# Another order of the block products, and of the sums before them, in the first and last of four matrix stages

## The chip, the cores and the metric

One Trainium2 chip, one core. The metric is the device time of one execution in microseconds (us), the median of several runs. TensorE (PE in the profile) multiplies and has its own row for loading weights (PEld); VectorE (DVE) and ScalarE (ACT) work elementwise; GpSimd (POOL) and SyncE (SP) mostly issue DMAs here.

## The reference

`x` is 2048 x 1024. Two branches are mixed row by row with a gate:

```python
g = _sigmoid((x * gate_w).sum(-1, keepdims=True))
# branch A
a = jnp.einsum("bsd,ed->bse", x, dft_hid_re)
b = jnp.einsum("bsd,ed->bse", x, dft_hid_im)
A = jnp.einsum("ts,bse->bte", dft_seq_re, a) - jnp.einsum("ts,bse->bte", dft_seq_im, b)
# branch B
h = _layernorm(x, axis=-1)
u = _gelu(jnp.einsum("bsd,sf->bdf", h, w1) + b1)
B = (jnp.einsum("bdf,fs->bds", u, w2) + b2).transpose(0, 2, 1)
return g * A + (1 - g) * B
```

The hidden width F is 3584; everything is float32.

## The kernel before, in words

Four large matrix products run one after the other as four stages, each a class: **Fourier** (name `q`: the sequence transform applied to x), **Mixed** (`y`: the hidden transform, written to the output with gate and bias), **Up** (`u`: layernormed x times w1, then gelu) and **Down** (`o`: u times w2, added onto the output with the gate). Fourier comes first and Down last; both the results of Fourier (`q`) and of Up (`u`) go through DRAM to the stage behind.

Each stage sees its product as a 4 x 4 grid of big blocks (16 of them) times a 4 x 2 grid of small blocks (8), which gives 8 output blocks. Instead of the 32 block products of the ordinary rule it takes the 26 of a fast scheme in the manner of Strassen. SCHEME (L49) has a row for each: which big blocks, with sign, are summed for one operand, which small ones for the other, and to which output blocks the product is added. ORDER is the order in which a stage takes the 26 rows, SUMS names partial sums that may be made on the way to an operand.

`plan` (L522) goes through the rows in that order. It makes each needed sum out of two that are at hand, choosing the cheapest pair: a block or sum that was used within the last `keep` products is still in SBUF; an older sum was stored to DRAM when made and is loaded again; a block of the input is loaded again. Where two rows in a row have the same small operand (`again`, L601), its split is kept. So the order decides how many loads, stores and sums there are and when each falls due.

Each operand is split (`split_into`, L508) into a high part, made by ScalarE (L509), and a low part, the rest, made by VectorE (L514 or L516), so that three float32r matmuls of 128 x 128 by 128 x 512 (L775 to L777) stand for a float32 product. The sums are VectorE's (`add` L479, `sub` L482); in Mixed and Down a few are made by an accumulating DMA issued from POOL (`add_onto`, L490). A product is 4 x 4 x 2 x 3 = 96 matmuls in Fourier and 7 x 4 x 3 = 84 in Down. In Fourier the big operand is 1024 wide and the small one 512, in Down both are 512; a sum or a split of a product takes four instructions in Fourier (4 slices of the contraction) and seven in Down.

A product runs through its slices k, over all its PSUM banks at each (8 in Fourier, 4 in Down, of 8 there are); the last two slices are taken together. Where the output signs of a product and of the next one agree enough, the next goes on in the same banks (`chained`, L613 to L619), and only the output blocks whose coefficient changes are read in between (`reads`, L620). A read is a first copy into SBUF by ScalarE or VectorE, whichever is free (`plain_copy`, L812 or L814), or an add onto the block by VectorE (`fused`, L820), one instruction a bank. A block that isn't read again for more than `gap` products is finished: in Fourier stored (L495), or accumulated onto its stored first part by DMA (L900); in Down scaled by ScalarE (L1037) and accumulated onto the output by DMA (L1039), but for those which the last product ends: they are loaded, added onto with the gate as scale, and stored by SP.

The order of all instructions is fixed when the kernel is built. Graph (L284) holds every load, sum, split, matmul group, copy and store as a task with a key, roughly its due time in slices, and the engines that can do it; `schedule` (L323) plays them through with an assumed duration for each, takes the ready task with the lowest key on each engine, and gives out the buffers: 40 of 128 x 1024 ("f"), 23 of 128 x 512 ("h") and 8 PSUM banks. The matmuls keep the order in which they are built. Loads go through SP's queue, most stores and all accumulating DMAs through POOL's. In product 1 of Fourier the saved sums are stored by SP. From product 12 of Fourier on, the statistics of the 16 row tiles of x are made beside it (`STATS_AT`, L206).

Of the kernel before, what the change touches and what calls it, by code (L numbers as in the profile page):

```python
# [44 lines left out]
def signs(words):  # L45
    return [[(c == "+") - (c == "-") for c in word] for word in words]
# [54 lines left out]
    '.-.-...+',  # L101
    '..+--+..',
])
Q_ORDER = [5, 14, 23, 3, 7, 11, 21, 22, 18, 24, 6, 17, 0, 13, 9, 8, 19, 15, 12, 2, 20, 25, 1, 16, 10, 4]
Q_SUMS = signs([
    '+.+.............',
    '.............+.+',
# [7 lines left out]
    '.....+.......+..',  # L115
    '+...........+...',
    '......+...+.....',
    '.+.+............',
    '.+.+.....+......',
    '.+.+.--...-.....',  # L120
    '.+.+.....+.+....',
    '....+...+.......',
    '....+-..+....-.-',
    '....+..++.......',
    '....+..++..+....',
    '+-..........+..+',
    '+-.......-..+..+',
    '......+...+.+..+',
    '......+...+.+.++',
    '....+..+........',  # L130
    '+.+.-..-..+.....',
    '..+.......+..+.+',
    '..+.......+..+++',
]), SMALL_SUMS
Q_PERM = ((0, 1, 2, 3), (0, 1, 2, 3), (0, 1))
# [69 lines left out]

STATS_AT, STATS_STEP = ("q", 12), 3  # L206
H_LEAD, H_EACH = 25, 1.3
O_ORDER = [24, 6, 17, 15, 0, 13, 12, 2, 25, 1, 16, 10, 5, 14, 4, 23, 3, 7, 11, 21, 18, 22, 9, 8, 19, 20]
O_SUMS = signs([
    '+.+.............',  # L210
    '.............+.+',
# [7 lines left out]
    '.....+.......+..',  # L219
    '+...........+...',  # L220
    '......+...+.....',
    '....+...+.......',
    '....+-..+....-.-',
    '....+..++.......',
    '....+..++..+....',
    '.+.+............',
    '.+.+.....+......',
    '.+.+.--...-.....',
    '.+.+.....+.+....',
    '..+.......+...+.',  # L230
    '..+.......+..+++',
    '....+..+........',
    '+.+.-..-..+.....',
    '............+.++',
    '......+...+.+.++',
    '+........-..+..+',
    '+-.......-..+..+',
]), SMALL_SUMS


# [171 lines left out]
def gated_mix_kernel(  # L412
# [411 lines left out]
    class Fourier(Bilinear):  # L824
        gap = Q_GAP

        def __init__(self):
            super().__init__("q", 4, 4, 2, H, D, "R", {"R": 1, "W": 2}, Q_ORDER, Q_SUMS, Q_PERM)

# [163 lines left out]
    class Down(Bilinear):  # L993
# [4 lines left out]
        def __init__(self):  # L998
            super().__init__("o", 7, 4, 1, H, H, "W", {"W": O_KEEP, "R": O_KEEP}, O_ORDER, O_SUMS, O_PERM)

# [197 lines left out]
```

## Time and profile before

| | |
|---|---|
| median of 3 runs | 1852.84 us (1852.65 to 1852.87) |
| profiled execution, its own time | 1853.4 us |
| span from its first to its last instruction | 1851.6 us |
| instructions | 24397 |
| granted TensorE clock | 1.000 |
| DMA | 491.88 MB, 266 GB/s mean |
| Fourier, about | 5 to 570 us |
| Down, about | 1352 to 1847 us |

The profile is of one execution. An engine's busy time counts its own instructions, not the issuing of DMAs by SP or the waits. Rows of groups give line, engine, operation, output and inputs, shape and count, then busy us and mean ns of one, then the idle time before them and what ended most of it. Rows of windows give for a stretch of time its length, then the busy us and the instructions of PE, PEld, DVE, ACT and POOL, the granted clock, the busy share of the DMA engines, and GB/s. Rows of a timeline give start and duration in us. Matmuls are pipelined: the starts are the ones to go by.

### The profile page before, as it was taken

The page shows a single profiled execution, that of the slowest core. Times are in us where ns is not written, and L with a number is a line of the kernel's source. Part 1 is how long each engine was busy: PE and PEld are TensorE (multiplying, and loading weights), DVE is VectorE, ACT ScalarE, POOL GpSimd, SP SyncE. Part 2 cuts the span into 40 slices and gives each one's busy share as a digit, 9 for nine tenths or more (in the row PEclk, how much of TensorE's full clock was granted, in tenths as well). Part 3 has the DMA queues.
Part 4 walks back from the last instruction along what each step waited for, and adds up shares of the span by engine and source line. Part 5 has one row for each costly group of instructions (what it writes and reads, how often), then busy time and mean ns, then how long its engine had stood idle before and what let it go on. Part 6 is the DMA issues. An engine that isn't in the chain of part 4 may idle for free.

```text
span 1851.6 us, 24397 instructions
## 1 busy us (share of the span) xinstructions
PE 1845.6 (100%) x8122; PEld 1524.0 (82%) x8122; DVE 1684.5 (91%) x2444; ACT 911.4 (49%) x1406; POOL 244.1 (13%) x416
## 2 busy tenths in 40 slices
PE   9999999999999999999999999999999999999999
PEld 7888888888888888888888888888888888888887
DVE  8899679989979999999988699899789999998995
ACT  5443335644535545586554325345455535444542
POOL 0100010111022101112121111121120000001111
PEclk9999999999999999999999999999999999999999
DMA  9967478879698667989658798796998576775974
GB/s 372 343 238 265 145 259 315 325 266 393 212 315 303 224 224 238 328 289 343 230 189 290 258 356 326 272 399 230 351 317 276 168 205 210 228 208 134 280 203 97
DMA packets 199870, 491.88 MB, mean 266 GB/s; under 512 B 24832, under 2 KB 24832, under 8 KB 199744
## 3 DMA queue, kind: packets, MB, share of 16 engines
q1 hardware_dynamic: 161712, 373.91, 58.5%
q0 software_dynamic: 37888, 116.16, 19.3%
q8 instruction: 63, 1.03, 0.2%
q14 instruction: 63, 0.52, 0.1%
q10 hardware_dynamic: 144, 0.26, 0.0%
HBM read 375.41 MB, written 114.82 MB: 265 GB/s over the span
## 4 chain that ended last, share of the span: by engine, by line
PE 84%; DVE 6%; issue 4%; DMA 4%; POOL 1%; SPq 0%; ACT 0%; POOLq 0%; DVEq 0%; ACTq 0%
PE ps_q_p L777 10%; PE ps_q_p L775 10%; PE ps_q_p L776 10%; PE ps_u_p L775 9%; PE ps_u_p L777 9%; PE ps_u_p L776 9%; PE ps_o_p L775 7%; PE ps_o_p L777 7%; PE ps_o_p L776 7%; PE ps_y_p L775 2%; PE ps_y_p L777 2%; PE ps_y_p L776 2%; DMA o_W_p<-in_w_dram 2%; DMA y_W_p<-y_W 1%; DVE o_p_r L516 1%
## 5 line engine op out<-in xcount | busy, mean ns | idle before, releaser
L777 PE MATMUL ps_q_p<-q_p_r_hi,q_p_w_lo 128*128 128x512 f32 x824 | 320.7, 389 | 0.1
L775 PE MATMUL ps_q_p<-q_p_r_hi,q_p_w_hi 128*128 128x512 f32 x824 | 320.6, 389 | 0.0
L776 PE MATMUL ps_q_p<-q_p_r_lo,q_p_w_hi 128*128 128x512 f32 x824 | 320.5, 389 | 0.0
L775 PE MATMUL ps_o_p<-o_p_r,o_p_w 128*128 128x512 f32 x728 | 283.5, 389 | 0.1
L776 PE MATMUL ps_o_p<-o_p_r,o_p_w 128*128 128x512 f32 x728 | 283.2, 389 | 0.0
L777 PE MATMUL ps_o_p<-o_p_r,o_p_w 128*128 128x512 f32 x728 | 283.2, 389 | 0.0
L775 PE MATMUL ps_u_p<-u_p_r_hi,u_p_w_hi 128*128 128x512 f32 x728 | 283.2, 389 | 0.0
L776 PE MATMUL ps_u_p<-u_p_r_lo,u_p_w_hi 128*128 128x512 f32 x728 | 283.2, 389 | 0.0
L777 PE MATMUL ps_u_p<-u_p_r_hi,u_p_w_lo 128*128 128x512 f32 x728 | 283.2, 389 | 0.0
L777 PEld LDWEIGHTS ps_q_p<-q_p_r_hi,q_p_w_lo 128*128 128x128 f32 x824 | 154.7, 188 | 32.7 <-DVE q_p_w_lo L514 0.6
L776 PEld LDWEIGHTS ps_q_p<-q_p_r_lo,q_p_w_hi 128*128 128x128 f32 x824 | 154.7, 188 | 32.1
L775 PEld LDWEIGHTS ps_q_p<-q_p_r_hi,q_p_w_hi 128*128 128x128 f32 x824 | 154.7, 188 | 32.0
L509 ACT ACTIVATE q_p_r_hi<-q_R_p 128x1024 fp32r<-128x1024 f32 (+1 forms) x101 | 104.4, 1047 | 132.6 <-DVE q_R_p L479 75.7
L509 ACT ACTIVATE o_p_w<-o_W_p 128x512 fp32r<-128x512 f32 x182 | 111.5, 627 | 113.3 <-DVE o_W_p L479 42.7
L509 ACT ACTIVATE u_p_w_hi<-u_W_p 128x896 fp32r<-128x896 f32 x104 | 97.5, 949 | 135.1 <-DVE u_W_p L479 95.2
L775 PE MATMUL ps_y_p<-y_p_r,y_p_w 128*128 128x512 f32 x416 | 162.2, 390 | 0.6 <-ACT y_c L812 0.4
L777 PE MATMUL ps_y_p<-y_p_r,y_p_w 128*128 128x512 f32 x416 | 161.9, 389 | 0.0
L776 PE MATMUL ps_y_p<-y_p_r,y_p_w 128*128 128x512 f32 x416 | 161.9, 389 | 0.0
L775 PEld LDWEIGHTS ps_o_p<-o_p_r,o_p_w 128*128 128x128 f32 x728 | 136.7, 188 | 29.3 <-DVE o_c L820 1.0
L776 PEld LDWEIGHTS ps_o_p<-o_p_r,o_p_w 128*128 128x128 f32 x728 | 136.7, 188 | 28.5
L777 PEld LDWEIGHTS ps_u_p<-u_p_r_hi,u_p_w_lo 128*128 128x128 f32 x728 | 136.7, 188 | 28.5
L776 PEld LDWEIGHTS ps_u_p<-u_p_r_lo,u_p_w_hi 128*128 128x128 f32 x728 | 136.7, 188 | 28.3
(149 smaller groups left out, 3260.7 us busy)
## 6 DMA issues: line engine op xcount, KB each, us to landing
q_R_p<-in_ct_dram SPq DMA_DIRECT2D x131, 512.0 KB, 7.1
u_W_p<-in_w_dram SPq DMA_DIRECT2D x136, 448.0 KB, 6.4
o_W_p<-in_w_dram SPq DMA_DIRECT2D x196, 256.0 KB, 5.3
o_R_p<-u SPq DMA_DIRECT2D x140, 256.0 KB, 5.0
u<-u_c POOLq DMA_DIRECT2D x126, 256.0 KB, 5.9
y_W_p<-q SPq DMA_DIRECT2D x99, 256.0 KB, 5.2
q<-q_c POOLq DMA_DIRECT2D x80, 256.0 KB, 5.6
q_W_p<-in_x_dram SPq DMA_DIRECT2D x75, 256.0 KB, 6.9
```

Source lines behind the costliest of these rows:

```text
L509: g.add({"ACT": act(v.n)}, key, lambda e: nc.scalar.activation(hi.ap, v.ap, AF.Copy, scale=-1.0 if negate else 1.0), r=(v.reg,), w=(hi.reg,))
L516: nc.vector.tensor_sub(lo.ap, v.ap, hi.ap.bitcast(F32))
L775: nc.tensor.matmul(bank.ap, wh.ap[:, c], rh.ap[:, e], start=a, stop=False, skip_group_check=True)
L776: nc.tensor.matmul(bank.ap, wh.ap[:, c], rl.ap[:, e], start=False, stop=False, skip_group_check=True)
L777: nc.tensor.matmul(bank.ap, wl.ap[:, c], rh.ap[:, e], start=False, stop=b, skip_group_check=True)
```

## The change

Q_ORDER with Q_SUMS, for Fourier, and O_ORDER with O_SUMS, for Down, are replaced; nothing else is. The scheme, the number of products, the matmuls, the tiles, the keep and gap values and the two middle stages' tables stay as they are. In Fourier rows 24, 6, 17, 15 come first, then 5, 14, 23, 3, 7, 11; the last eight rows (12 to 4) keep their places. In Down the order is new from the first row to the last. The partial sums that differ are those that suit the new order.

```diff
--- before.py
+++ after.py
@@ -101,7 +101,7 @@
     '.-.-...+',
     '..+--+..',
 ])
-Q_ORDER = [5, 14, 23, 3, 7, 11, 21, 22, 18, 24, 6, 17, 0, 13, 9, 8, 19, 15, 12, 2, 20, 25, 1, 16, 10, 4]
+Q_ORDER = [24, 6, 17, 15, 5, 14, 23, 3, 7, 11, 21, 18, 22, 9, 8, 19, 0, 13, 12, 2, 20, 25, 1, 16, 10, 4]
 Q_SUMS = signs([
     '+.+.............',
     '.............+.+',
@@ -115,21 +115,21 @@
     '.....+.......+..',
     '+...........+...',
     '......+...+.....',
-    '.+.+............',
+    '.+.......+......',
     '.+.+.....+......',
-    '.+.+.--...-.....',
     '.+.+.....+.+....',
+    '+-.......-..+..+',
     '....+...+.......',
     '....+-..+....-.-',
     '....+..++.......',
     '....+..++..+....',
-    '+-..........+..+',
-    '+-.......-..+..+',
-    '......+...+.+..+',
+    '...+.--...-.....',
+    '.+.+.--...-.....',
+    '............+.++',
     '......+...+.+.++',
     '....+..+........',
     '+.+.-..-..+.....',
-    '..+.......+..+.+',
+    '.............+++',
     '..+.......+..+++',
 ]), SMALL_SUMS
 Q_PERM = ((0, 1, 2, 3), (0, 1, 2, 3), (0, 1))
@@ -205,7 +205,7 @@
 
 STATS_AT, STATS_STEP = ("q", 12), 3
 H_LEAD, H_EACH = 25, 1.3
-O_ORDER = [24, 6, 17, 15, 0, 13, 12, 2, 25, 1, 16, 10, 5, 14, 4, 23, 3, 7, 11, 21, 18, 22, 9, 8, 19, 20]
+O_ORDER = [5, 0, 13, 14, 23, 4, 17, 24, 6, 19, 15, 3, 7, 11, 21, 22, 9, 8, 20, 12, 2, 25, 1, 16, 10, 18]
 O_SUMS = signs([
     '+.+.............',
     '.............+.+',
@@ -219,22 +219,22 @@
     '.....+.......+..',
     '+...........+...',
     '......+...+.....',
-    '....+...+.......',
-    '....+-..+....-.-',
+    '....+..+........',
+    '+.+.-..-..+.....',
     '....+..++.......',
     '....+..++..+....',
     '.+.+............',
     '.+.+.....+......',
     '.+.+.--...-.....',
     '.+.+.....+.+....',
-    '..+.......+...+.',
+    '+..+........+..+',
+    '+-.......-..+..+',
+    '....+-.......-.-',
+    '....+-..+....-.-',
+    '.............+++',
     '..+.......+..+++',
-    '....+..+........',
-    '+.+.-..-..+.....',
     '............+.++',
     '......+...+.+.++',
-    '+........-..+..+',
-    '+-.......-..+..+',
 ]), SMALL_SUMS
 
 
```

## The prediction

> **What bounds the kernel now.** I read the page first, then TensorE's timeline from end to end, then the time windows, then the timelines of VectorE around each place where TensorE stopped. The page:
>
> ```profile
> span 1851.6 us, 24397 instructions
> PE 1845.6 (100%) x8122; PEld 1524.0 (82%) x8122; DVE 1684.5 (91%) x2444; ACT 911.4 (49%) x1406; POOL 244.1 (13%) x416
> ```
>
> TensorE is busy all the time, but ends of matmuls are modelled, so I look at the starts instead. TensorE's timeline (start, duration, line) at the beginning and at the end; 54 rows lie between the last two:
>
> ```profile
> 1.19 4.45 PE L1133 MATMUL pw<-warm 128*128 128x512 bf16 x10 [1.19 <-DVE warm L1131]
> 5.25 1.66 PE L876 MATMUL ps_q_p<-q_p_r_hi,q_p_w_hi 128*128 128x512 f32 x4
> ...
> 1834.76 0.39 PE L776 MATMUL ps_o_p<-o_p_r,o_p_w 128*128 128x512 f32 x1
> ...
> 1847.22 0.39 PE L777 MATMUL ps_o_p<-o_p_r,o_p_w 128*128 128x512 f32 x1
> ```
>
> In 12.46 us there are 55 steps: 0.2266 us a matmul. The program has 26 products of 96 + 48 + 84 + 84 matmuls, 8112 besides the 10 of the warm-up, so 8111 steps from 5.25 take at least 1838 us and would end at 1843.3; the last starts at 1847.2. **About 4 us** is all that TensorE loses between its first and last real matmul. Three of the stops lie in the stages that change (Fourier and Down); for each, the matmul before and after it:
>
> ```profile
> 39.42 0.39 PE L776 MATMUL ps_q_p<-q_p_r_lo,q_p_w_hi 128*128 128x512 f32 x1
> 39.95 0.50 PE L777 MATMUL ps_q_p<-q_p_r_hi,q_p_w_lo 128*128 128x512 f32 x1
> ...
> 1486.74 0.39 PE L777 MATMUL ps_o_p<-o_p_r,o_p_w 128*128 128x512 f32 x1
> 1487.14 0.50 PE L775 MATMUL ps_o_p<-o_p_r,o_p_w 128*128 128x512 f32 x1
> ...
> 1791.70 0.39 PE L777 MATMUL ps_o_p<-o_p_r,o_p_w 128*128 128x512 f32 x1
> 1792.19 0.50 PE L775 MATMUL ps_o_p<-o_p_r,o_p_w 128*128 128x512 f32 x1
> ```
>
> Start to start less 0.227, and 0.11 for the longer next one (0.50 for 0.39): 0.41, 0.28 and 0.37 us, **1.1 us together**. The rest is in Mixed, as the groups of weight loads show (last figure: idle time before them, and its releaser):
>
> ```profile
> L775 PEld LDWEIGHTS ps_y_p<-y_p_r,y_p_w 128*128 128x128 f32 x416 | 78.1, 188 | 18.1 <-DVE y_c L820 1.0 <-ACT y_c L812 0.9
> L777 PEld LDWEIGHTS ps_y_p<-y_p_r,y_p_w 128*128 128x128 f32 x416 | 78.1, 188 | 16.3
> ```
>
> 18.1 less 16.3 is 1.8 us, waits for an evacuation of PSUM. So the kernel is bound by TensorE's count of matmuls, which no order changes. A gain is at most the 1.1 us of Fourier and Down, or 2.9 with Mixed. The start (first loads and splits, to 5.25) and the end keep their shapes.
>
> **The two ways in which TensorE can stop.** Operands late (39.95), or an evacuation late. A "chained" product goes on in the PSUM banks of the one before; where those are also read, it must wait for the readers. VectorE around the stop at 1487.14:
>
> ```profile
> 1481.61 2.48 DVE L820 SCALAR_TENSOR_TENSOR o_c<-ps_o_p,o_c 128x512 f32<-128x512 f32 x4
> 1484.00 0.68 DVE L514 SCALAR_TENSOR_TENSOR o_p_w<-o_W_p,o_p_w 128x512 fp32r<-128x512 f32 x1
> 1484.60 2.48 DVE L820 SCALAR_TENSOR_TENSOR o_c<-ps_o_p,o_c 128x512 f32<-128x512 f32 x4
> ```
>
> Two blocks of four banks are added onto; the last add ends at 1487.08, and the matmul starts at 1487.14. I place it by counting 19.04 us a product (84 x 0.2266) back from the end: it opens product 7 of Down.
>
> **Is VectorE close to the bound?** Busy time by stage, then two full slices, then the POOL, ACT and DVE groups that I use:
>
> ```profile
> 5.00:570.00 565.00, 564.86 (x2489) 467.30 (x2488) 504.96 (x652) 267.48 (x402) 63.95 (x113) 1.00 0.80 290
> 1352.40:1847.40 495.00, 494.88 (x2182) 408.93 (x2180) 461.89 (x759) 235.86 (x400) 48.50 (x64) 1.00 0.72 212
> ```
>
> ```profile
> 113.00:135.00 22.00, 22.00 (x99) 18.23 (x98) 22.00 (x30) 9.36 (x14) 0.54 (x1) 1.00 0.71 238
> 1390.40:1409.50 19.10, 19.10 (x86) 15.71 (x85) 19.10 (x32) 14.41 (x26) 1.09 (x2) 1.00 0.83 270
> ```
>
> ```profile
> L495 POOL DMA_DIRECT2D q_W<-q_W_p x16 | 8.9, 554 | 203.2 <-DVE q_W_p L482 191.8 <-DVE q_W_p L479 11.1
> L900 POOL DMA_DIRECT2D q<-q_c x8 | 6.8, 856 | 14.8 <-ACT q_c L812 14.2 <-DVE q_c L814 0.6
> L495 POOL DMA_DIRECT2D o_W<-o_W_p x7 | 3.8, 543 | 6.7 <-DVE o_W_p L479 6.2 <-DVE o_R_p L482 0.2 <-issue 0.2
> L490 POOL DMA_DIRECT2D o_W_p<-in_w_dram x14 | 12.4, 886 | 259.3 <-DMA o_c<-out_dram 60.0 <-DVE o_p_w L514 47.9 <-DVE o_p_w L516 35.3
> L812 ACT ACTIVATE o_c<-ps_o_p 128x512 f32<-128x512 f32 x23 | 13.7, 597 | 16.2 <-PE ps_o_p L777 15.9
> L814 DVE TENSOR_SCALAR o_c<-ps_o_p 128x512 f32<-128x512 f32 x5 | 3.5, 690 | 1.5 <-ACT o_c L812 1.1 <-PE ps_o_p L777 0.4
> L820 DVE SCALAR_TENSOR_TENSOR q_c<-ps_q_p,q_c x168: 679/686/693, 84.1 to 572.6; 128x512 f32<-128x512 f32 x168
> ```
>
> VectorE is spare for 60 us of 565 in Fourier and 33 us of 495 in Down. Filled, it ends 32 instructions of Down in 19.10 us, **0.60 us each** though each lasts 0.69; a 1024-wide one costs about twice, say 1.14. In 113 to 135 VectorE has no idle time and TensorE loses none: operands are made ahead, and what counts is by how much.
>
> **The change, part by part.** The counts come from the rules of plan (L522) and operand (L691), followed over both sets of tables.
>
> Fourier: sums 72 and 112 as before. Input loads fall from 76 to 72 (256 KB) and 132 to 128 (512 KB), reloads of saved sums from 28 to 20 and 20 to 16, their stores from 24 to 16 and 20 to 16. Blocks added onto in SBUF fall from 168 instructions to 160 (8 x 0.60 = 4.8 us of VectorE less); first copies rise from 72 to 88, shared by ACT and VectorE. Two more blocks are written in two parts, so accumulating DMAs rise from 8 to 24: 16 x 0.86 = 13.7 us of POOL, less 8 saved-sum stores there at 0.55, so +9.3 on 64 busy of 565. Behind them in POOL's queue stand other stores of blocks and sums. Products 18 to 25 keep their order, so every block that Mixed reads ends where it did, block 0 one product earlier. VectorE's demand, summed product by product, differs from before by 0 through product 2, -18 to -28 us at 4, 6 and 7, +9.6 at most (12), then -4 to -14. Counting 21.76 us a product from 5.25, the last operand of product 12 is made 28 us ahead now, and the nearest misses are product 1 (the stop at 39.95) and product 15:
>
> ```profile
> 340.39 0.69 DVE L516 TENSOR_TENSOR q_p_w_lo<-q_W_p,q_p_w_hi 128x512 fp32r<-128x512 f32 x1
> ```
>
> It ends 1.5 us before use (342.6), and becomes 14 us easier. Fourier therefore keeps its 0.41 (products 0 and 1 have the same shape) and gains no stop.
>
> Down: sums on VectorE 182 + 125 become 186 + 126, adds onto blocks 104 become 108: +9 x 0.60 = **5.4 us of 33 spare**. Saved sums stored 21 -> 35, loaded 21 -> 35, input loads 210 + 140 -> 210 + 126, sums made by DMA 15 -> 10. On POOL that is 14 x 0.543 less 5 x 0.886, +3.2 us on 48.5; behind these in its queue are only other stores and the accumulations of finished blocks. DMA engines are 0.72 busy there. The demand in instructions per product (seven a sum, seven a split, four a block added from the product before) is now 14, 42, 20, 21, 24, 44, 25, 36, 37, 21, 38, 28, 18, 32, 29, 24, 24, 38, 29, 36, 30, 34, 25, 31, 31, 36; it becomes 14, 21, 44, 31, 25, 21, 38, 18, 32, 45, 21, 24, 38, 29, 36, 32, 21, 25, 36, 21, 36, 38, 25, 38, 31, 36. At 32 a product VectorE is full. The running difference is 7.8 and 8.4 us at products 3 and 4, 9.6 at 15, 5.4 at 23 to 25. Against it stand the leads. The last low half of W of product 1, and the last of all 182:
>
> ```profile
> 1379.22 0.68 DVE L514 SCALAR_TENSOR_TENSOR o_p_w<-o_W_p,o_p_w 128x512 fp32r<-128x512 f32 x1
> ...
> 1825.73 0.68 DVE L516 TENSOR_TENSOR o_p_w<-o_W_p,o_p_w 128x512 fp32r<-128x512 f32 x1
> ```
>
> They are used 13.6 us into products 1 and 25, at 1384.8 and 1841.8: leads of 4.9 and 15.4. The same count over all 26 gives 10 to 31 elsewhere. Subtracting the running difference, the smallest leads after are 9.3 (product 2), 10 (3) and **8.8** (24). No operand comes late.
>
> What is left in Down is evacuation. Chained products that follow a reading: 14 now, 16 after; at 0.65 us for 14 that is 0.75. New is one of **three** blocks, after product 0: twelve copies of 0.60. TensorE's last pass takes 1.36 us a bank and its next needs bank 3 at 7.5 us from that pass's start. ACT and VectorE together, three copies a bank in under 1.36, end at about 7.2 (no cost); ACT alone ends at 1.4 + 7.2 = 8.6 (1.1 late). I take 0.4.
>
> Sum: -0.41 + 0.41 in Fourier, 0 in Mixed and Up, +0.1 + 0.4 in Down: span 1852.1. The profiled execution took 1853.4 for its 1851.6; the median of the runs is 1852.84, which I move by the same 0.5: **1853.3 us**.
>
> [...] POOL issues more DMAs, and its busy rows stand above. [...]
>
> **Rivals.** (1) *Slower by the triple copy.* If ACT does its usual share (23 of 28 copies now, so 9.6 of 12) with a split between every two, it ends 1.4 + 9.6 x 1.2 = 12.9 us after the pass began: 5.4 late, **1858.3**. It decides once copies end later than 7.5. For: VectorE's queue at 1484 did put a split between the adds. Against: the two-block copy after product 1 shows no stop. Chance 0.12. (2) *Slower by a hole in the loads.* VectorE runs short in Down even now:
>
> ```profile
> 1676.00:1695.10 19.10, 19.10 (x86) 15.82 (x85) 17.27 (x30) 8.74 (x15) 3.83 (x5) 1.00 0.68 135
> 1695.10:1714.10 19.00, 19.00 (x85) 15.74 (x84) 14.92 (x25) 7.49 (x12) 0.98 (x2) 1.00 0.40 127
> 1714.10:1733.20 19.10, 19.10 (x85) 15.80 (x85) 17.27 (x29) 11.59 (x19) 3.99 (x5) 1.00 1.00 259
> 1733.20:1752.20 19.00, 19.00 (x85) 15.76 (x84) 17.62 (x30) 8.30 (x15) 2.76 (x4) 1.00 1.03 294
> ```
>
> That is 1.8 + 4.1 + 1.8 + 1.4 = 9.1 us idle in a row. The same at products 1 to 4 or 21 to 24 is just covered by 8.8; one twice as deep costs 18.2 - 8.8 = 9.4, **1862.7**. It decides above 8.8. Against: fewer blocks are open at once (6 for 8 in Down, 5 for 6 in Fourier), which leaves more buffers for loads. Chance 0.16. (3) *Faster:* all stops of Fourier and Down go, **1851.8**; with Mixed's, 1849.9. Still within 0.2%. Chance 0.12. My forecast, with small stops moved about: 0.60.
>
> **Numbers.** 0.2% (3.7 us) is about what a measurement of this kernel can tell from no change. Faster by more needs more than the 2.9 us of stops that exist: 0.02, out of (3), for what I don't see. Slower by more is (1) and (2): 0.28. Within: 0.70. The range goes from 1850.8, most of Fourier's, Mixed's and Down's stops gone, to 1860, which takes in (1) and the smaller holes of (2); about 0.15 is left out. The forecast's own range is 1851.8 to 1855.
>
> **What would show it.** Right: starts 0.227 apart throughout, stops only at chained boundaries, the count of L900 at 24, DVE's instructions in Down up by 9, o_W stores 28. Wrong: a stop of more than 1 us at 1371 (triple copy), or one ended by a split's low half in products 2 to 4 or 21 to 25 of Down (a lead that I overrated), or any stop in Fourier after product 2.

## The result, and the profile after

The changed kernel takes **1856.24 us** (median of 22 runs, 1854.58 to 1859.10), the kernel before 1852.67 (22 runs, 1852.13 to 1853.92): a ratio of 1.0021, with a 95% interval from 1.0015 to 1.0027. That is 3.6 us: slower clear of the noise, at the very edge of the 0.2% (3.7 us) that the prediction set as its bound, and seven times the 0.5 us that it forecast. The spread has grown from 1.8 to 4.5 us, which the forecast did not have at all. The first profile of the changed kernel is of its fastest execution: 1854.58 us, span 1852.8.

The head of its page, then the groups whose counts were forecast:

```profile
span 1852.8 us, 24399 instructions
PE 1845.2 (100%) x8122; PEld 1523.1 (82%) x8122; DVE 1694.1 (91%) x2463; ACT 908.4 (49%) x1404; POOL 255.7 (14%) x433
```

```profile
L900 POOL DMA_DIRECT2D q<-q_c x24 | 20.6, 863 | 84.4 <-DVE q_c L820 69.6 <-ACT q_c L812 14.6 <-issue 0.2
L495 POOL DMA_DIRECT2D o_W<-o_W_p x28 | 15.2, 545 | 87.3 <-DVE o_W_p L479 70.9 <-DMA o_W_p<-in_w_dram 12.7 <-DVE o_Ws L479 3.6
```

The work is what was counted: 24 accumulating stores in Fourier, 28 stores of saved sums of w2 in Down. The time has gone elsewhere. TensorE's timeline at its beginning (the warm-up, then the first product) and in the first pass of Down's product 1, where banks 2 and 3 are taken over from product 0:

```profile
1.19 4.45 PE L1133 MATMUL pw<-warm 128*128 128x512 bf16 x10 [1.19 <-DVE warm L1131]
6.33 1.19 PE L876 MATMUL ps_q_p<-q_p_r_hi,q_p_w_hi 128*128 128x512 f32 x4 [0.69 <-ACT q_p_r_hi L509]
...
1371.50 0.39 PE L777 MATMUL ps_o_p<-o_p_r,o_p_w 128*128 128x512 f32 x1
1372.18 0.50 PE L775 MATMUL ps_o_p<-o_p_r,o_p_w 128*128 128x512 f32 x1 [0.29 <-ACT o_c L812]
1372.52 0.40 PE L776 MATMUL ps_o_p<-o_p_r,o_p_w 128*128 128x512 f32 x1
1372.76 0.40 PE L777 MATMUL ps_o_p<-o_p_r,o_p_w 128*128 128x512 f32 x1
1374.11 0.50 PE L775 MATMUL ps_o_p<-o_p_r,o_p_w 128*128 128x512 f32 x1 [0.95 <-DVE o_c L814]
```

Two things stand out against before. The first real matmul starts at 6.33 us where it started at 5.25. And after product 0 of Down TensorE stops twice, for 0.68 - 0.23 + 0.11 = 0.56 and 1.35 - 0.23 + 0.11 = 1.23 us: **1.8 us** at the copy of three blocks. Before's stops at 39.95, 1487 and 1792 are gone, and the last matmul starts at 1848.25 for 1847.22. So this execution is 1.0 us behind the profiled one of before, while the medians are 3.6 apart: before's profiled execution (1853.4) was 0.7 over its median and this one 1.7 under its own. The rest must be in what differs from one execution to the next.

### The profile page after: what moved, and what is told of

Same layout as the page of the kernel before. It is cut to its first block, busy times and chain, and to the rows that moved or that the text cites. A ratio compares the mean times of both kernels' runs of the same rounds, so it can differ in the third digit from the quotient of the medians.

```text
span 1852.8 us, 24399 instructions
## 1 busy us (share of the span) xinstructions
PE 1845.2 (100%) x8122; PEld 1523.1 (82%) x8122; DVE 1694.1 (91%) x2463; ACT 908.4 (49%) x1404; POOL 255.7 (14%) x433
## 4 chain that ended last, share of the span: by engine, by line
PE 99%; DVE 1%; ACT 0%; DMA 0%; issue 0%; ACTq 0%
PE ps_q_p L777 10%; PE ps_q_p L776 10%; PE ps_q_p L775 10%; PE ps_u_p L775 9%; PE ps_u_p L777 9%; PE ps_u_p L776 9%; PE ps_o_p L775 9%; PE ps_o_p L776 9%; PE ps_o_p L777 9%; PE ps_y_p L775 5%; PE ps_y_p L776 5%; PE ps_y_p L777 5%; PE ps_q_p L876 0%; DMA q_W_p<-in_x_dram 0%; DVE o_c L814 0%; ACT o_c L812 0%
## 5 line engine op out<-in xcount | busy, mean ns | idle before, releaser
L509 ACT ACTIVATE q_p_r_hi<-q_R_p 128x1024 fp32r<-128x1024 f32 (+1 forms) x105 | 108.9, 1049 | 126.2 <-DVE q_R_p L479 88.2
L775 PEld LDWEIGHTS ps_u_p<-u_p_r_hi,u_p_w_hi 128*128 128x128 f32 x728 | 136.6, 188 | 28.3
```

The costliest lines, as they stand in the source:

```text
L509: g.add({"ACT": act(v.n)}, key, lambda e: nc.scalar.activation(hi.ap, v.ap, AF.Copy, scale=-1.0 if negate else 1.0), r=(v.reg,), w=(hi.reg,))
L775: nc.tensor.matmul(bank.ap, wh.ap[:, c], rh.ap[:, e], start=a, stop=False, skip_group_check=True)
```

## The experiments

Two theories were tried against each other: **A**, that the loss lies in Down, in the triple copy; **B**, that it lies in Fourier, and varies. All times below are medians of 10 or 11 runs; the kernel before ran beside each group of four (1852.44, 1852.44 and 1852.72 us). The 95% interval of a ratio to it is about 0.0009 to either side, 1.7 us, so a difference of 1 to 2 us between two medians is at the edge of what the times alone can tell; it is the profiles that show where it arises.

**Each half of the change alone, the whole once more.** The tables of one stage were put into the kernel before:

```diff
-Q_ORDER = [5, 14, 23, 3, 7, 11, 21, 22, 18, 24, 6, 17, ...
+Q_ORDER = [24, 6, 17, 15, 5, 14, 23, 3, 7, 11, 21, 18, ...      (q_only, with its Q_SUMS)
```

```diff
-O_ORDER = [24, 6, 17, 15, 0, 13, 12, 2, 25, 1, 16, 10, ...
+O_ORDER = [5, 0, 13, 14, 23, 4, 17, 24, 6, 19, 15, 3, ...       (o_only, with its O_SUMS)
```

> Only Fourier has its new tables; Down keeps its old ones. Theory A (the cost lies in Down, at the copy of three blocks after product 0): the time is that of before within 0.5 us (1852.2 to 1853.2), no stop at 1371 us and stops of 0.3 to 0.4 at Down's products 7 and 23 as before. Theory B (Fourier costs it, by operands or loads that come late in some executions): 2 to 3.5 us above before, with a wide spread from run to run, and stops of TensorE between 5 and 570 us.

> Only Down has its new tables; Fourier keeps its old ones. Theory A: 1.5 to 3.5 us above before, with TensorE's stop of about 1.8 us after product 0 of Down. Theory B: within 1.3 us of before, since the 1.8 us of that stop stand against 0.65 us of old ones that are gone.

> The changed kernel once more, for a second profile beside the first (1854.58 us, the fastest of its 22 runs, median 1856.24). Theory A: 1854.5 to 1857, and the second profile shows the stop of about 1.8 us at 1371 us again. Theory B: a profile of a slower execution shows, besides, a stop of 1 to 4 us in Fourier that the first profile does not have.

Measured: only Fourier 1853.81 (1852.52 to 1857.61), only Down 1854.45 (1853.53 to 1854.96), both 1856.22 (1855.51 to 1858.14). Against 1852.44 that is +1.4, +2.0 and +3.8: within the noise the halves add up, and neither theory has it all. Down's half is steady, Fourier's carries the spread. The second profile of the changed kernel, of 1856.73 us, shows where, on TensorE's timeline:

```profile
1.19 4.45 PE L1133 MATMUL pw<-warm 128*128 128x512 bf16 x10 [1.19 <-DVE warm L1131]
6.51 2.08 PE L876 MATMUL ps_q_p<-q_p_r_hi,q_p_w_hi 128*128 128x512 f32 x4 [0.87 <-ACT q_p_r_hi L509]
8.38 1.84 PE L876 MATMUL ps_q_p<-q_p_r_lo,q_p_w_hi 128*128 128x512 f32 x4
10.06 1.09 PE L876 MATMUL ps_q_p<-q_p_r_hi,q_p_w_lo 128*128 128x512 f32 x4
```

Not only does the first matmul start late: the first eight take 3.55 us, 0.44 each, where eight take 1.81 at 0.227 and took 2.43 in the profile of before. So B was right that Fourier's loss varies, and wrong on where: no operand in the middle of the stage is late, it is all in the first 10 us. That execution's sum: start +1.26, slow matmuls +1.12 more than before's, the triple copy +1.79, less 0.41 for the stop at 39.95, less 0.84 in Mixed, +0.29 in the rest of Down: 3.2, and its last matmul starts 3.2 us after before's, at 1850.41.

**Who makes the three copies.** ScalarE's and VectorE's timelines of the changed kernel (its first profile) around the stop show why it is over four times as long as the 0.4 us assumed:

```profile
1366.49 0.60 ACT L812 ACTIVATE o_c<-ps_o_p 128x512 f32<-128x512 f32 x1 [4.32 <-PE ps_o_p L777]
1367.84 1.09 ACT L812 ACTIVATE o_c<-ps_o_p 128x512 f32<-128x512 f32 x2 [0.76 <-DVE o_c L814]
1369.69 1.09 ACT L812 ACTIVATE o_c<-ps_o_p 128x512 f32<-128x512 f32 x2 [0.76 <-DVE o_c L814]
1371.53 0.60 ACT L812 ACTIVATE o_c<-ps_o_p 128x512 f32<-128x512 f32 x1 [0.76 <-DVE o_c L814]
...
1372.73 0.60 ACT L812 ACTIVATE o_c<-ps_o_p 128x512 f32<-128x512 f32 x1
```

```profile
1367.12 0.69 DVE L814 TENSOR_SCALAR o_c<-ps_o_p 128x512 f32<-128x512 f32 x1 [3.57 <-ACT o_c L812]
...
1368.96 0.69 DVE L814 TENSOR_SCALAR o_c<-ps_o_p 128x512 f32<-128x512 f32 x1 [0.56 <-ACT o_c L812]
...
1370.81 0.69 DVE L814 TENSOR_SCALAR o_c<-ps_o_p 128x512 f32<-128x512 f32 x1 [0.55 <-ACT o_c L812]
...
1372.01 0.69 DVE L814 TENSOR_SCALAR o_c<-ps_o_p 128x512 f32<-128x512 f32 x1
1373.36 0.69 DVE L814 TENSOR_SCALAR o_c<-ps_o_p 128x512 f32<-128x512 f32 x1 [0.66 <-ACT o_c L812]
```

The releasers alternate. The copies of one bank go to ScalarE, VectorE, ScalarE, and each waits for the one before, on the other engine: 1366.49, 1367.12, 1367.84 for the first, and a bank takes 1.85 us (1367.12 to 1368.96 to 1370.81) while TensorE fills one in 1.36. The last copy ends 9.1 us after TensorE's last pass began (1364.93), where 7.5 was needed. In each 1.85 us ScalarE stands idle for 0.76 and VectorE for 0.55. In the kernel's own Graph, readers of one bank do not depend on each other, so the schedule did not foresee these waits; what puts them in, no run here shows. No two copies of one bank overlap in the trace: each starts 0.03 to 0.04 us after the one before it has ended (1366.49 + 0.60 to 1367.12, 1367.12 + 0.69 to 1367.84). The edit keeps the work and gives each bank to one engine (not shown: the lines that make `only` a parameter and keep the product's number in `self.j`; m is the bank):

```diff
-            plain_copy(key, o, ps, float(coef))
+            plain_copy(key, o, ps, float(coef), ("ACT", "DVE")[m % 2] if self.j == 0 else None)
...
-        g.add({"ACT": act(o.n), "DVE": dve(o.n)}, key, go, r=(ps.reg,), w=(o.reg,))
+        cost = {"ACT": act(o.n), "DVE": dve(o.n)}
+        g.add({only: cost[only]} if only else cost, key, go, r=(ps.reg,), w=(o.reg,))
```

> The changed kernel, but the three copies of one bank after product 0 of Down all go to one engine: banks 0 and 2 to ScalarE, 1 and 3 to VectorE. In the changed kernel's profile the two engines' copies of one bank wait for each other in turn, 1.85 us a bank, against a matmul pass of 1.36 us a bank. Theory A (this chain is the stop): copies of neighbouring banks overlap, the stop falls from 1.78 to under 0.5 us, and the time by 1.3 to 1.8. Rival (three copies of a bank are too many whoever makes them, or VectorE's other work is in the way): the stop stays at 1.5 us or more and the time is that of the changed kernel within 0.5 us.

Measured: 1854.41, 1.8 us under the changed kernel beside it. ScalarE's and VectorE's timelines, then TensorE's:

```profile
1366.72 1.58 ACT L812 ACTIVATE o_c<-ps_o_p 128x512 f32<-128x512 f32 x3 [4.32 <-PE ps_o_p L777]
1369.44 1.58 ACT L812 ACTIVATE o_c<-ps_o_p 128x512 f32<-128x512 f32 x3 [1.14 <-PE ps_o_p L777]
```

```profile
1368.08 1.89 DVE L814 TENSOR_SCALAR o_c<-ps_o_p 128x512 f32<-128x512 f32 x3 [3.70 <-PE ps_o_p L777]
...
1370.80 1.89 DVE L814 TENSOR_SCALAR o_c<-ps_o_p 128x512 f32<-128x512 f32 x3 [0.23 <-PE ps_o_p L777]
```

```profile
1372.41 0.39 PE L777 MATMUL ps_o_p<-o_p_r,o_p_w 128*128 128x512 f32 x1
1372.74 0.50 PE L775 MATMUL ps_o_p<-o_p_r,o_p_w 128*128 128x512 f32 x1
```

Three copies run back to back and wait for TensorE only, and what is left of the stop is 0.2 us. The other way to take the alternation out, with one engine only, tells it from a shortage of engines:

```diff
-("ACT", "DVE")[m % 2] if self.j == 0
+"ACT" if self.j == 0
```

> The changed kernel, but all twelve copies after product 0 of Down go to ScalarE. Theory A (the stop comes from the change of engines within a bank, one wait for the other at each step): back to back on one engine a bank takes 3 x 0.54 = 1.6 us, the last bank is read out 7.9 us after TensorE's last pass began against 7.5 needed, so the stop falls from 1.78 to 0.3 to 0.9 us and the time by 0.9 to 1.5. Rival (too few engines): with half the engines the stop grows to 3 us or more and the time rises by 1 us or more.

```profile
1367.29 5.99 ACT L812 ACTIVATE o_c<-ps_o_p 128x512 f32<-128x512 f32 x12 [4.17 <-PE ps_o_p L777]
```

Measured: 1853.87 (1853.18 to 1857.07), a stop of 0.2 us. The stop is even a little shorter than theory A expected; the time is 2.2 us under the changed kernel's 1856.08 of the last run below, more than the stop explains and within the noise of two medians. Twelve copies on one engine, back to back, take 5.99 us, less than the same twelve shared out over two (1366.49 to 1374.05, 7.6 us). The chain was the stop.

**Why the first matmul is late.** It waits for its operands' high halves, and those for the first loads. In the profiles with the new tables of Fourier so far the first load of x takes longer though its size, queue and place in the queue are the same. The DMA issues of the first 13 us, before the change and after it (size, us from issue to landing):

```profile
q_R_p<-in_ct_dram SPq DMA_DIRECT2D x2, 256.0 KB, 3.6
q_W_p<-in_x_dram ACTq DMA_DIRECT2D x1, 256.0 KB, 3.3
```

```profile
q_R_p<-in_ct_dram SPq DMA_DIRECT2D x2, 256.0 KB, 4.3
q_W_p<-in_x_dram ACTq DMA_DIRECT2D x1, 256.0 KB, 4.4
```

Only the source differs: row 24 of the scheme begins with columns 0 to 511 of rows 512 to 639 of x, row 5 began with columns 512 to 1023 of rows 0 to 127. Three edits of Q_PERM, which renames blocks and leaves every product, sum and count as it is, tell columns from rows:

```diff
-Q_PERM = ((0, 1, 2, 3), (0, 1, 2, 3), (0, 1))
+Q_PERM = ((0, 1, 2, 3), (0, 1, 2, 3), (1, 0))      (other_half, in the changed kernel; before_half, in the one before)
+Q_PERM = ((0, 1, 2, 3), (1, 0, 2, 3), (0, 1))      (other_rows, in the changed kernel)
```

> The changed kernel with the two column halves of x changed over in Fourier (the last part of Q_PERM), so that its first load from x takes columns 512 to 1023, as before the change, of rows 512 to 639, which before took rows 0 to 127. With the new Fourier tables that load lands after 4.4 to 4.5 us in four profiles, with the old ones after 3.3 in two, and TensorE starts at 6.3 to 6.6 instead of 5.25. Theory H (the column half decides: columns 0 to 511 of x and of the transform are fetched at once and get in each other's way): 3.3 us to landing, first matmul at about 5.25, 1.2 to 2 us faster than the changed kernel. Theory R (the row block decides): 4.4 us, first matmul at 6.3 or later, the time of the changed kernel within 0.5 us.

> The changed kernel with the first two row blocks of the contraction changed over in Fourier (the middle part of Q_PERM): its first loads take rows 0 to 127 of x and of the transform's slab, as before the change, but columns 0 to 511 of x. Theory H: 4.4 us to landing, first matmul at 6.3 or later, the changed kernel's time within 0.5 us. Theory R: 3.3 us, first matmul at 5.25, 1.2 to 2 us faster than the changed kernel.

> The kernel before the change with the two column halves of x changed over in Fourier: the same products, sums and loads, but the first load from x takes columns 0 to 511 of rows 0 to 127. Theory H: the load lands after 4.4 us, TensorE starts at 6.3 or later, 1.2 to 2 us slower than before with a spread of some us. Theory R: no change, 3.3 us, 5.25, within 0.5 us of before.

The same two rows of the DMA issues, for other_half, then other_rows, then before_half:

```profile
q_R_p<-in_ct_dram SPq DMA_DIRECT2D x2, 256.0 KB, 3.6
q_W_p<-in_x_dram ACTq DMA_DIRECT2D x1, 256.0 KB, 3.4
```

```profile
q_R_p<-in_ct_dram SPq DMA_DIRECT2D x2, 256.0 KB, 4.6
q_W_p<-in_x_dram ACTq DMA_DIRECT2D x1, 256.0 KB, 4.6
```

```profile
q_R_p<-in_ct_dram SPq DMA_DIRECT2D x2, 256.0 KB, 4.5
q_W_p<-in_x_dram ACTq DMA_DIRECT2D x1, 256.0 KB, 4.4
```

Measured: 1855.02 (1.2 us under the changed kernel's 1856.22), 1856.20 (no change) and 1853.80 (1.4 us over the kernel before, which computes the same sums in the same order). First matmuls at 5.33, 6.59 and 6.40 us. The column half decides when the load lands, the rows don't, and the order of the products doesn't either. The loads of the transform that run at the same time are slowed with it, by 0.7 to 1.0 us; they begin with columns 0 to 511 too. That the two loads meet somewhere on the way from DRAM fits this, but where, no run here shows.

**Is anything else lost?** Each stage's new tables with its own mend (q_other_half, o_mended), and both together (both_mended, which has the rows of other_rows as well, so that its first loads are where before's were):

> Only Fourier has its new tables, with the column halves of x changed over as in other_half; Down keeps its old ones. Theory A with H (Fourier's new order costs nothing but its late first load): first matmul at about 5.3, no stop at 39 us, 1851.9 to 1853.0, the time of before within 0.6 us. Rival (the order itself costs something in Fourier or in Mixed behind it): 1853.3 or more with the first matmul at 5.3 all the same.

> Only Down has its new tables, with one engine per bank for the copies after product 0; Fourier keeps its old ones. Theory A (Down's new order costs nothing but the chain of copies): no stop over 0.5 us in Down, 1852.2 to 1853.0. Rival (the operands or the other evacuations of Down's new order cost too): 1853.5 to 1854.5, as o_only less at most 1 us.

> The changed kernel with one engine per bank for the copies after product 0 of Down, and with rows and column halves of Fourier permuted so that its first loads are at the addresses of before. Theory A with H or R (the whole loss is the late first load, with TensorE's slow clock behind it, and the triple copy): first matmul at 5.25, no stop over 0.5 us at 1371, and 1851.8 to 1853.2, at or just under the time of before. Rival (another 1 us or more of loss lies in the new orders, in Fourier's POOL queue or Down's operands): 1853.5 to 1855.

Measured: Fourier 1852.43 against 1852.72 (ratio 0.9999, interval 0.9991 to 1.0008), Down 1853.14 against 1852.72 (1.0002, 0.9993 to 1.0011), both 1852.75 against 1852.44 (1.0005, 0.9996 to 1.0013). All three are the same as before within their intervals; Down's 1853.14 is 0.1 over the range that theory A gave it. The two new orders as such are neutral as far as this can tell (a loss of 0.13%, 2.4 us, would still lie within the widest interval). Of the 3.8 us, 0.3 are left in the median: the column half of one load and the alternation within four banks were nearly the whole loss. None of these beats the kernel before.

One kind of loss is left that these edits don't touch. In seven of the ten profiles with Down's new tables TensorE also waits 0.5 us or more where product 8, 10 or 18 of Down opens, for VectorE to read a bank that it takes over. In other_half, at product 8:

```profile
1506.59 0.50 PE L775 MATMUL ps_o_p<-o_p_r,o_p_w 128*128 128x512 f32 x1 [0.34 <-DVE o_c L820]
1506.92 0.39 PE L776 MATMUL ps_o_p<-o_p_r,o_p_w 128*128 128x512 f32 x1
1507.15 0.40 PE L777 MATMUL ps_o_p<-o_p_r,o_p_w 128*128 128x512 f32 x1
1507.79 0.50 PE L775 MATMUL ps_o_p<-o_p_r,o_p_w 128*128 128x512 f32 x1 [0.24 <-DVE o_c L820]
```

That is 1.1 us. The old tables have such stops at products 7, 17 and 23 (0.2 to 0.5 us). The same instructions have them in one execution and not in another, and Mixed, whose tables are the same in all, loses between 0.8 and 2.7 us in the fourteen profiles; why, no run here shows.

**The slow first matmuls.** The last run tried to close the idle time between warm-up and first product:

```diff
-        for n in range(10):
+        for n in range(12):
```

> The changed kernel with 12 warm-up matmuls instead of 10, so that TensorE is busy until about 6.3 us and does not idle for 0.7 to 1.1 us before its first real matmul. In the slower profiles the first eight matmuls take 0.47 us each instead of 0.23, in the faster ones only the first. Theory C (the idle time before the first matmul keeps TensorE at half its rate for longer): the spread (10 executions from 1855.5 to 1858.1) narrows to under 1.5 us and the median falls by 0.5 to 1.5 us. Rival (the half rate depends on something that the warm-up doesn't touch, such as when the execution begins): the same median and spread within 0.4 us.

Measured: 1856.08, 1854.58 to 1857.16. The median is that of the changed kernel, and so is the spread (2.6 us, as in the ten runs of after_again): theory C's gain did not come. But the run tells less than was hoped: in its profile the end of the warm-up already runs fast, the warm-up ends at 6.0 and not at 6.3, and 0.60 us of idle time remain.

Fourteen profiles of all these kernels show two rates at the start: matmuls begin 0.43 us apart, and from some moment 0.23 or less. Where the first product starts by 5.6 us (six profiles), the fast rate holds from its start or from 6.3 to 6.9. Where it starts at 6.3 or later, after idle time, the fast rate holds from its start (five profiles) or only from about 10 (three profiles, with 1.6 to 1.7 us lost). The moment is not tied to the start of the work: in q_other_half it falls into the warm-up, whose ten matmuls take 3.70 us and not 4.45:

```profile
1.20 3.70 PE L1133 MATMUL pw<-warm 128*128 128x512 bf16 x10 [1.20 <-DVE warm L1131]
```

What sets the moment, no run here shows. It is no fixed time after the work begins: counted from the first matmul of the warm-up, the fast rate comes after 2.8 us in q_other_half, by the starts of its matmuls, and after 8.9 in after_again (10.06 less 1.19), where TensorE stands idle for 0.87 us in between. So a late start cost more than its own delay in three of those eight profiles, by 1.6 to 1.7 us, and no more than it in five. That is argued from fourteen profiles and not shown by an edit.

## Why the prediction was right or wrong

*Right: TensorE's count is the bound, no gain over 0.2%, no loss from operands.* The running differences of VectorE's demand gave the leads to within 4 us. Smallest leads forecast for Down were 9.3 us (product 2), 10 (3) and 8.8 (24). The last low half of W of product 3 in the changed kernel:

```profile
1416.18 0.68 DVE L514 SCALAR_TENSOR_TENSOR o_p_w<-o_W_p,o_p_w 128x512 fp32r<-128x512 f32 x1
```

It is used at 1424.1, counting 19.04 us a product back from the last matmul: 7.2 us ahead. Counted so, product 2 has 7.6 and product 24 has 12.8, and no lead of Down in the changed kernel is under 7. Rival (2), a hole in the loads, did not come: no stop of Down with its new tables was for an operand, in any of the profiles. (A hole of 9.1 us is not quite "covered by 8.8", as the prediction has it; it would cost 0.3.) Nor do POOL's further DMAs (433 instructions of POOL for 416) show in the length of VectorE's instructions: its sums out of two SBUF inputs in Down last 685 ns in the changed kernel, and 684 in the one before:

```profile
L482 DVE TENSOR_TENSOR o_R_p<-o_R_p,o_R_p 128x512 f32<-128x512 f32 x85 | 58.1, 685 | 0.0
```

*Right: Fourier's new order costs its stage nothing and POOL's 16 more accumulating stores cost nothing* (q_other_half, within its interval). Its stop at 39.95 was to stay and went. In the profile of before the last low half of product 1 ends at 39.90, 0.4 us too late for its matmul; with the new tables and the early start of q_other_half it ends at 39.12, 0.3 us ahead of its matmul at 39.44. SP's queue then stores 8 saved sums beside that product instead of 12, which may be why; with the old tables and a late start (before_half) the stop is gone too.

*Mis-sized: "I take 0.4" for the three-block copy.* Place and mechanism, an evacuation that ends late at a chained boundary, were right, and so was the sign by which to know it, a stop over 1 us at 1371. It measured 1.8. The step that failed, in the prediction's words, is "ACT and VectorE together, three copies a bank in under 1.36": here two engines on one bank are slower than one, they hand over at each copy, 1.85 us a bank against 1.58 on ScalarE. With ScalarE alone the prediction had 1.1 us late and it is 0.2; the case that it took for safe was the bad one. Rival (1) had the right place too, but priced a split between every two of ScalarE's copies, and there was one (at 1372.02), in a time when ScalarE had to wait for VectorE anyway.

*Wrong: "The start (first loads and splits, to 5.25) and the end keep their shapes", and products 0 and 1 "have the same shape".* Their counts and sizes are the same, their addresses are not, and those made the first load 1.1 us slower; with the slow matmuls behind it that is +1.4 us in the median and much of the spread. The prediction did not ask which columns the first load reads, and the trace of before had only the good case. So the range held the time (1856.24 within 1850.8 to 1860), but the median lies outside the forecast's own range of 1851.8 to 1855. That it held is in part luck: the upper part of the range was meant for rivals (1) and (2), neither of which came as described, and a loss that the prediction had at nothing, the late start, brought the time there.

## What to carry to other kernels

Where an engine is full from end to end, as TensorE is here, look for the cost of a change of order at the seams (here 1.8 us at the triple copy, and 1.4 in the median at the first loads): at the first loads, the first matmuls and each place where the full engine must wait for a reader of its results, and price those one by one. Give the copies out of one PSUM bank to one engine: here that worked both with neighbouring banks on different engines and with all banks on one (a stop of 0.2 us in each, where it was 1.8). When runs spread more after a change than before, take a second profile of a slower execution before explaining the median with the first.

## What was not expected of the hardware

Two loads of 256 KB, of x and of the transform, each with rows 4 KB apart of which 2 KB are read, landed after 4.3 to 4.7 us when both began in the same column half (eight profiles), and after 3.3 to 3.8 when x began in the other (six); the rows made no difference. Twelve ScalarE copies out of PSUM back to back took 0.50 us each, though one alone shows 0.60. And the granted clock in the profile's rows (the 1.00) stays at full while matmuls are 0.44 us apart, as in the slow beginning of after_again, so the start-to-start time, not that column, shows it, and where the expectation of both_mended speaks of a "slow clock", these starts are all that was measured:

```profile
6.51:10.06 3.55, 3.55 (x9) 2.84 (x9) 3.06 (x5) 2.64 (x4) 0.00 (x0) 1.00 1.04 389
```
